# One projection of q instead of two, its features turned by DMA, and kv rows of 66 numbers

## The chip, the cores and the metric

The kernel runs on one core of a Trainium2 chip. The metric is device time in microseconds (us) of one execution; a kernel's time is the median of several executions. A core has five engines that each take their own list of instructions in order: TensorE (PE in the profile; its weight loads are PEld), VectorE (DVE), ScalarE (ACT), GpSimd (POOL) and SyncE (SP). Waits between engines go over semaphores. Transfers are carried by 16 DMA engines; here POOL issues the loads, SP the transposes and the stores.

## The reference

Linear attention with learned features, then a two-layer network with a squared ReLU. Batch 8, 8 heads, 576 positions, head size 64, 128 features; the network is 512 to 2048 to 512 over all 4608 tokens.

```
def phi(x):
    proj = einsum('bhsd,df->bhsf', x, w_phi)
    proj = proj - max(abs(proj), axis=-1, keepdims=True)
    return concatenate([exp(proj), exp(-proj)], axis=-1)
q_p, k_p = phi(q), phi(k)
kv  = einsum('bhsf,bhsd->bhfd', k_p, v)
z   = sum(k_p, axis=2)
num = einsum('bhsf,bhfd->bhsd', q_p, kv)
den = einsum('bhsf,bhf->bhs', q_p, z) + 1e-6
x   = (num / den), heads side by side    # (4608, 512)
out = (max(x @ w_in, 0) ** 2) @ w_out
```

## The kernel before

**Attention, one batch after another.** `attention(b)` handles the 576 positions of a batch as chunks of 128 positions and one of 64, for 8 heads. From batch 2 on, k and q are turned by one DMA transpose each (`transposed`, L326: `kT`, `qT`, 18 blocks of 128x128 each, issued by SP); in batches 0 and 1 TensorE turns them (L316).

For k, a group is projected onto the features (operation Pk, L342, half-height matmuls that run two at a time), DVE takes the largest absolute value (Mk, L397) and ACT makes exp(x) and exp(-x) (Ekp, Ekn, L403, tiles `kp` and `kn`, a ring of `NKP` slots). The maximum goes into `va`, the scaled v, whose rows have room for 66 numbers: 64 of v, the scale that gives the denominator, and one spare. `kv_ops` multiplies `kp` and `kn` with `va` into PSUM (L458, L463), and operation kvc copies the result to `kv_sb`, in rows of 65 numbers (`D1`), 64 of kv and one of z.

For q the projection is made twice. `qmax_ops` projects with the positions on the partitions (Pq, L342), DVE takes the maximum (Mq, L500), and ACT makes exp(-2 max) of it (en). `q_ops` projects once more with the features on the partitions (Fq, L535: two matmuls of 64 rows by 512 columns), and ACT makes exp(x) and exp(-x) from that (L550, tiles `qp` and `qn`). `out_ops` multiplies these with `kv_sb`: eight matmuls with `qp` (NA, L614), the scaling by en on DVE (SA, L626), eight with `qn` on top (NB, L614), a reciprocal (rd, L636), the division (xo, L640), and from batch 1 on a DMA transpose of the result on SP (Xx, L674: `xT`, or `xS` for the chunk of 64), 4 blocks.

**The network.** The 4608 tokens are nine chunks of 512: chunk c is the first 512 positions of batch c, and the ninth is the last 64 positions of all eight batches, collected in `xS`. The first layer is L755 (F1; for chunk 0 the smaller forms f1a, f1b, f1 and f1p at L766, L780 and L794), the ReLU is made by ACT (L732) or DVE (L734), the square by DVE (L741). The second layer is L849 (F2; L813 for the last tile), followed by a copy `ot` on ACT or DVE (L192, L190) and a store on SP (L867, L864).

**The order.** The program makes 1738 operations, each with an engine and planned costs, and then issues them in the order of a list of their numbers, `ORDER`. Each engine's instructions are tied to each other in that order, so the list sets what stands behind what on every engine. `BASES` gives each operation its PSUM bank, `STATES` says for each copy and ReLU whether ACT or DVE makes it, `GATES` makes each load of batch 2 and later on POOL wait for a named operation, and `FILL` puts matmuls on a zero tile (L922, `warm`) ahead of some operations at the start. These tables are the result of an offline search over the planned costs.

Of the kernel before, what the change touches and what calls it, by code (L numbers as in the profile page):

```python
# [107 lines left out]
def kernel(  # L108
# [55 lines left out]
    NKP = 7  # L164
# [4 lines left out]
    kv_sb = ring("kv", 2, [4, 2, 2, D1])  # L169
    NQP = 3  # L170
    NXT = 2
    assert B * S == NCH * TCH and NCH == B + 1 and S == TCH + 64
    qp, qn = ring("qp", NQP, [8 * P]), ring("qn", NQP, [8 * P])
# [4 lines left out]
    mkn = sb("mkn", [36], F32)  # L178
# [120 lines left out]
    kslot, qslot, xslot = [0], [0], [0]  # L299
# [4 lines left out]
    def attention(b):  # L304
# [146 lines left out]
        def kv_ops(pr):  # L451
# [20 lines left out]
            def fn():  # L472
                copy(kv_sb[s2][:, pr].rearrange("f s h c -> f (s h c)"), ps1(g)[:, : 4 * D1])
# [11 lines left out]
        def qmax_ops(c):  # L485
# [17 lines left out]
            add("DVE", dve_cost(2 * n * Fd), fn, r=[pj], w=[("mq", s2, c)], closes=pj, what="Mq")  # L503

# [13 lines left out]
        qfeat = {}  # L518

        def q_ops(c):  # L520
# [21 lines left out]
            for sgn, dst, nm in ((1.0, qp, "qp"), (-1.0, qn, "qn")):  # L542
                def fn(dst=dst, sgn=sgn):
                    i_ = ps2(pf)[:, :, : n * P]
                    if c == 4:
                        o = dst[slot][:, : 8 * 64].rearrange("f (i e x) -> f e i x", e=2, x=P)
                        i_ = i_.rearrange("f e (i x) -> f e i x", x=P)
                    else:
                        o = dst[slot].rearrange("f (e x) -> f e x", e=2)
                    pin(nc.scalar.activation(out=o, in_=i_, func=ACT.Exp, scale=sgn))  # L550
                add("ACT", act_cost(2 * n * P), fn, r=[pf], w=[pf, (nm, slot)],
                    closes=pf if sgn < 0 else None, what="E" + nm)

        def out_halves():
# [4 lines left out]
            for hf in range(2):  # L559
                g = Bank(1, "b0")  # L560
                def heads(sg, g=g, hf=hf):
                    def fn():
                        for u in range(4):
                            h = 4 * hf + u
                            pin(nc.tensor.matmul(
                                out=ps1(g)[:, u * D1 : (u + 1) * D1], lhsT=(qp, qn)[sg][slot][:, h * P : (h + 1) * P],
                                rhs=kv_sb[s2][:, h // 2, sg, h % 2, :], start=(sg == 0 and u == 0),
                                stop=(sg == 1 and u == 3), skip_group_check=True))
                    return fn
# [3 lines left out]
                add("PE", pe_cost(4, 0.0313), heads(0), r=[("qp", slot)] + kvs, w=[g], opens=g, what="NAh")  # L573
# [4 lines left out]
                add("PE", pe_cost(4, 0.0313), heads(1), r=[("qn", slot)] + kvs, w=[g], what="NBh")  # L578
# [21 lines left out]
        def out_ops(c):  # L600
# [4 lines left out]
            slot = qfeat[c]  # L605
# [3 lines left out]
            def heads(sg):  # L609
                def fn():  # L610
                    o = ps2(g)
                    for u in range(8):
# [3 lines left out]
                            lhsT=(qp, qn)[sg][slot][:, u * m : u * m + P],  # L616
                            rhs=kv_sb[s2][:, h // 2, sg, h % 2, :], start=(sg == 0 and u % 4 == 0),
# [3 lines left out]
            add("PE", pe_cost(8, 0.0313), heads(0), r=[("qp", slot)] + kvs, w=[g], opens=g, what="NA")  # L621
# [8 lines left out]
            add("PE", pe_cost(8, 0.0313), heads(1), r=[("qn", slot)] + kvs, w=[g], what="NB")  # L630
# [68 lines left out]
        else:  # L699
# [18 lines left out]
            for c in range(5):  # L718
                qmax_ops(c)
            for c in range(5):  # L720
                q_ops(c)
                out_ops(c)
# [351 lines left out]
```

## Time and profile before

| | |
|---|---|
| median of 3 runs | 353.51 us (353.29 to 354.12) |
| profiled execution, first to last instruction | 351.3 us |
| PE, DVE, ACT busy | 98%, 76%, 67% |
| POOL busy | 27% |
| packets of the loads (queue 0), share of 16 DMA engines | 45.1% |
| packets of SP's transposes and stores (queue 1), the same | 27.2% |
| granted TensorE clock | 1.00 |

The profiled execution is one of its own. The page gives its span, which is 2.2 us under the median of the runs; no other time of it is listed. A busy share is an average over the span. PE's instructions overlap in the pipeline, so what one costs PE is read from the start of one to the start of the next, not from its duration. The rows for SP and for DMA issues show when a transfer was issued and how long it took to land.

### The profile page before, as it was taken

The page shows a single profiled execution, that of the slowest core. Times are in us where ns is not written, and L with a number is a line of the kernel's source. Part 1 is how long each engine was busy: PE and PEld are TensorE (multiplying, and loading weights), DVE is VectorE, ACT ScalarE, POOL GpSimd, SP SyncE. Part 2 cuts the span into 40 slices and gives each one's busy share as a digit, 9 for nine tenths or more (in the row PEclk, how much of TensorE's full clock was granted, in tenths as well). Part 3 has the DMA queues.
Part 4 walks back from the last instruction along what each step waited for, and adds up shares of the span by engine and source line. Part 5 has one row for each costly group of instructions (what it writes and reads, how often), then busy time and mean ns, then how long its engine had stood idle before and what let it go on. Part 6 is the DMA issues. An engine that isn't in the chain of part 4 may idle for free.

```text
span 351.3 us, 8451 instructions
## 1 busy us (share of the span) xinstructions
PE 343.6 (98%) x3402; PEld 193.1 (55%) x3402; DVE 267.2 (76%) x511; ACT 234.9 (67%) x441; POOL 96.2 (27%) x144
## 2 busy tenths in 40 slices
PE   8899999999999999999999999999999999999995
PEld 6789667545655545446555544465555444444443
DVE  5999898999989997898868987998668532645610
ACT  4999998599787885687598857896675612431111
POOL 8827260584509701796013101000000000000000
PEclk9999999999999999999999999999999999999999
DMA  8999999999979999999559774102310113000114
GB/s 104 181 203 197 201 135 129 144 141 179 161 170 155 156 169 193 158 174 134 131 127 106 69 188 80 69 2 61 62 60 10 32 30 124 5 1 29 62 63 116
DMA packets 96117, 39.59 MB, mean 113 GB/s; under 512 B 64592, under 2 KB 91600, under 8 KB 96080
## 3 DMA queue, kind: packets, MB, share of 16 engines
q0 software_dynamic: 45232, 18.36, 45.1%
q1 hardware_dynamic: 50608, 20.55, 27.2%
q8 instruction: 26, 0.43, 0.6%
q10 hardware_dynamic: 240, 0.16, 0.2%
q14 instruction: 11, 0.09, 0.1%
HBM read 36.77 MB, written 9.44 MB: 132 GB/s over the span
## 4 chain that ended last, share of the span: by engine, by line
PE 76%; ACT 12%; DVE 7%; issue 2%; DMA 2%; DVEq 0%; ACTq 0%; POOLq 0%
PE psum L849 31%; PE psum L755 24%; PE psum L614 5%; PE psum L342 4%; PE psum L458 3%; ACT hr L732 2%; PE psum L535 2%; PE psum L794 2%; ACT kp L403 2%; DVE mk L397 2%; DVE h L741 1%; ACT kp L385 1%; DMA xT<-xo 1%; ACT kn L403 1%; ACT kn L385 1%
## 5 line engine op out<-in xcount | busy, mean ns | idle before, releaser
L849 PE MATMUL psum<-wout,h 128*128 128x512 bf16 x560 | 132.6, 379 | 0.1
L755 PE MATMUL psum<-xT,win 128*128 128x512 bf16 x448 | 105.6, 379 | 0.5 <-DVE hr L734 0.2
L732 ACT ACTIVATE hr<-psum 128x512 bf16<-128x512 f32 x101 | 58.3, 596 | 39.0 <-PE psum L755 20.9
L849 PEld LDWEIGHTS <-h 128*128 128x128 bf16 x560 | 51.0, 98 | 55.2 <-issue 0.8
L755 PEld LDWEIGHTS <-win 128*128 128x128 bf16 x512 | 47.2, 98 | 53.5 <-issue 3.4
L741 DVE TENSOR_TENSOR h<-hr 128x512 bf16<-128x512 bf16 x144 | 56.1, 417 | 10.6 <-ACT hr L732 9.6
L734 DVE TENSOR_SCALAR hr<-psum 128x512 bf16<-128x512 f32 x43 | 29.3, 686 | 26.8 <-PE psum L755 26.0
L500 DVE TENSOR_REDUCE mq<-psum 128x8 f32<-128x1024 f32 (+1 forms) x40 | 43.7, 1112 | 6.0 <-PE psum L342 5.7
L550 ACT ACTIVATE qp<-psum 128x1024 bf16<-128x1024 f32 (+1 forms) x40 | 37.5, 939 | 11.5 <-PE psum L535 7.1
L397 DVE TENSOR_REDUCE mk<-psum 128x8 f32<-128x1024 f32 (+1 forms) x35 | 38.6, 1112 | 6.8 <-PE psum L342 6.7
L403 ACT ACTIVATE kp<-psum 128x1024 bf16<-128x1024 f32 (+1 forms) x35 | 32.9, 939 | 15.4 <-DVE mk L397 15.2
L550 ACT ACTIVATE qn<-psum 128x1024 bf16<-128x1024 f32 (+1 forms) x40 | 37.4, 938 | 0.5 <-PE psum L614 0.4
L192 ACT ACTIVATE ot<-psum 128x512 f32<-128x512 f32 x25 | 14.7, 596 | 31.2 <-PE psum L849 29.4
L430 DVE TENSOR_TENSOR va<-xv,va 64x256 bf16<-64x256 bf16 (+2 forms) x66 | 29.8, 474 | 4.8 <-ACT va L416 2.1
L403 ACT ACTIVATE kn<-psum 128x1024 bf16<-128x1024 f32 (+1 forms) x35 | 32.7, 937 | 0.0
L245 POOL DMA_DIRECT2D xv<-in_v_dram x27 | 20.2, 757 | 44.7 <-DVE rden L636 19.1
L626 DVE TENSOR_TENSOR psum<-psum,en 128x520 f32<-128x520 f32 (+1 forms) x39 | 27.2, 699 | 5.3 <-PE psum L614 2.2
L640 DVE TENSOR_TENSOR xo<-psum,rden 128x512 bf16<-128x512 f32 (+1 forms) x39 | 26.7, 687 | 1.0
L245 POOL DMA_DIRECT2D xk<-in_k_dram x28 | 21.2, 768 | 3.6 <-ACT kp L403 2.8
L265 POOL DMA_DIRECT2D xq<-in_q_dram x24 | 17.7, 753 | 9.7 <-ACT qp L550 5.0
L458 PE MATMUL psum<-va,kp 128*128 128x65 bf16 x256 | 19.6, 193 | 0.2
L458 PE MATMUL psum<-va,kn 128*128 128x65 bf16 x256 | 19.6, 193 | 0.0
(82 smaller groups left out, 396.6 us busy)
## 6 DMA issues: line engine op xcount, KB each, us to landing
out_dram<-ot SPq DMA_DIRECT2D x32, 256.0 KB, 2.8
xk<-in_k_dram POOLq DMA_DIRECT2D x26, 128.0 KB, 4.5
xq<-in_q_dram POOLq DMA_DIRECT2D x24, 128.0 KB, 4.8
xv<-in_v_dram POOLq DMA_DIRECT2D x24, 128.0 KB, 4.4
win<-in_moe_w_in_dram POOLq DMA_DIRECT2D x4, 512.0 KB, 12.8
wout<-in_moe_w_out_dram POOLq DMA_DIRECT2D x4, 512.0 KB, 10.8
xq<-in_q_dram POOLq DMA_DIRECT2D x4, 256.0 KB, 6.9
out_dram<-ot SPq DMA_DIRECT2D x6, 128.0 KB, 2.3
```

Of the source, the lines that this page charges most:

```text
L245: pin(nc.gpsimd.dma_start(out=x[:, a * 512 : z * 512].rearrange("p (h x) -> p h x", x=4 * D), in_=src[b][2 * a : 2 * z, 0:512, :].rearrang ...
L397: pin(nc.vector.tensor_reduce(out=mk_view(g), in_=ps2(pj)[:, :, : n * Fd].rearrange("p e (i f) -> p e i f", f=Fd), axis=AX.X, op=ALU.max, ...
L403: pin(nc.scalar.activation(out=dst[slot][:, :, :n, :].rearrange("p e i f -> p e (i f)"), in_=ps2(pj)[:, :, : n * Fd], func=ACT.Exp, scale= ...
L430: pin(nc.vector.tensor_tensor(out=t[:, :, :D].rearrange("p m (x c) -> p m x c", c=2), in0=x.rearrange("p (m x c) -> p m x c", m=n, c=2), i ...
L458: pin(nc.tensor.matmul(out=o[:, sg, hi, :], lhsT=(kp, kn)[sg][kgroup[pr]][:, j % 2, 2 * hi + j // 2, :], rhs=va[s2][sg][:, 8 * pr + 4 * hi ...
L500: pin(nc.vector.tensor_reduce(out=mqb[:, c, :, :n], in_=ps2(pj)[:, :, : n * Fd].rearrange("p e (i f) -> p e i f", f=Fd), axis=AX.X, op=ALU ...
L550: pin(nc.scalar.activation(out=o, in_=i_, func=ACT.Exp, scale=sgn))
L732: pin(nc.scalar.activation(out=hr[sl], in_=ps1(g), func=ACT.Relu))
L734: pin(nc.vector.tensor_scalar(out=hr[sl], in0=ps1(g), scalar1=0.0, scalar2=None, op0=ALU.max))
L741: pin(nc.vector.tensor_tensor(out=dst, in0=i_, in1=i_, op=ALU.mult))
L755: pin(nc.tensor.matmul(out=o, lhsT=win[mc // 4][:, kc, mc % 4 * P : (mc % 4 + 1) * P], rhs=x, start=(kc == 0), stop=(kc == KC - 1)))
L849: pin(nc.tensor.matmul(out=ps1(g), lhsT=h2[c % 2][mc // 4][:, mc % 4, tt * P : (tt + 1) * P], rhs=wout[mc // 4][:, mc % 4, :], start=(mc = ...
```

## The change

From batch 2 on (`TURNED`), q is projected once, with the positions on the partitions. `q_turned` replaces `qmax_ops` and `q_ops` there: the same PSUM result goes to the maximum on DVE and to both exponentials on ACT, which write a tile `qf`, and SP issues a DMA transpose of `qf` into `qpn` (16 blocks of 128x128 for a chunk of 128 positions, 8 for the chunk of 64). `qp` and `qn` become two parts of one tile `qpn`. Batches 0 and 1 keep both projections.

The rows of `kv_sb` get 66 numbers, of which 65 are written and read. `NKP` goes from 7 to 6. The planned cost of one L614 matmul goes from 0.0313 to 0.0297. An unused tile, `mkn`, is dropped.

`ORDER`, `BASES`, `STATES`, `GATES` and `FILL` are new throughout. `FILL` holds 58 fillers where it held 142, and its first 26 stand ahead of another operation (85, a transpose of the last group of k, not 41, the first). POOL's first load is the second half of k of batch 0.

```
-    NKP = 7
+    NKP = 6
...
-    kv_sb = ring("kv", 2, [4, 2, 2, D1])
+    kv_sb = ring("kv", 2, [4, 2, 2, D1 + 1])
...
-    qp, qn = ring("qp", NQP, [8 * P]), ring("qn", NQP, [8 * P])
+    qf, qpn = ring("qf", NQF, [16 * P]), ring("qpn", NQP, [16 * P])     # NQF = 2, NQP = 3
...
-                copy(kv_sb[s2][:, pr].rearrange("f s h c -> f (s h c)"), ps1(g)[:, : 4 * D1])
+                copy(kv_sb[s2][:, pr].rearrange("f s h c -> f (s h) c")[:, :, :D1],
+                     ps1(g)[:, : 4 * D1].rearrange("f (n c) -> f n c", c=D1))
...
+        def q_turned(c):
+            ts = q_ts(c)
+            n = min(len(ts), 4)
+            f, slot = fslot[0] % NQF, qslot[0] % NQP
...
+            pj = project(qTb, "qT", ts, "Pq")
+            def fn():
+                pin(nc.vector.tensor_reduce(
+                    out=mqb[:, c, :, :n], in_=ps2(pj)[:, :, : n * Fd].rearrange("p e (i f) -> p e i f", f=Fd),
+                    axis=AX.X, op=ALU.max, apply_absolute_value=True))
+            add("DVE", dve_cost(2 * n * Fd), fn, r=[pj], w=[pj, ("mq", s2, c)], what="Mq")
+            for sgn, base in ((1.0, 0), (-1.0, 2 * n * P)):
+                def fn(sgn=sgn, base=base):
+                    i_ = ps2(pj)[:, :, : n * Fd]
+                    o = qf[f][:, base : base + 2 * n * P]
...
+                    pin(nc.scalar.activation(out=o, in_=i_, func=ACT.Exp, scale=sgn))
+                add("ACT", act_cost(2 * n * Fd), fn, r=[pj], w=[pj, ("qf", f, sgn)], closes=pj if sgn < 0 else None,
+                    what="Eqp" if sgn > 0 else "Eqn")
+            def fn():
+                pin(nc.sync.dma_start_transpose(out=qpn[slot][:, : 4 * n * P].rearrange("f (t x) -> f t x", x=P),
+                                                in_=qf[f][:, : 4 * n * P]))
+            add("SP", (0.78 + 0.44 * n, 0), fn, r=[("qf", f, 1.0), ("qf", f, -1.0)], w=[("qp", slot), ("qn", slot)],
+                dma=(0.47 * n, HW_IN, "x", "kq"), what="Xf")
+            en_ops(c)
...
-                            lhsT=(qp, qn)[sg][slot][:, u * m : u * m + P],
-                            rhs=kv_sb[s2][:, h // 2, sg, h % 2, :], start=(sg == 0 and u % 4 == 0),
+                            lhsT=qpn[slot][:, sg * half + u * m : sg * half + u * m + P],
+                            rhs=kv_sb[s2][:, h // 2, sg, h % 2, :D1], start=(sg == 0 and u % 4 == 0),
...
-            for c in range(5):
-                qmax_ops(c)
-            for c in range(5):
-                q_ops(c)
-                out_ops(c)
+            if b in TURNED:
+                for c in range(5):
+                    q_turned(c)
+                    out_ops(c)
+            else:
+                for c in range(5):
+                    qmax_ops(c)
+                for c in range(5):
+                    q_ops(c)
+                    out_ops(c)
...
+TURNED = range(2, 8)
```

More of the change, by code (lines that the diff above doesn't have):

```diff
@@ L168 @@
     en = ring("en", 2, [5, 8], F32)
-    kv_sb = ring("kv", 2, [4, 2, 2, D1])
+    kv_sb = ring("kv", 2, [4, 2, 2, D1 + 1])
     NQP = 3
+    NQF = 2
     NXT = 2
     assert B * S == NCH * TCH and NCH == B + 1 and S == TCH + 64
-    qp, qn = ring("qp", NQP, [8 * P]), ring("qn", NQP, [8 * P])
+    qf, qpn = ring("qf", NQF, [16 * P]), ring("qpn", NQP, [16 * P])
     xo = ring("xo", 3, [8 * D])
@@ L177 @@
     xS = sb("xS", [4, KC, P])
-    mkn = sb("mkn", [36], F32)
     hr = ring("hr", 4, [TCH])
@@ L296, in load_wout @@
         add("POOL", (0.72, 0), fn, w=[("wout", i)], dma=(LD["w"], SW_IN, "ld", "first"), what="wout")
-    kslot, qslot, xslot = [0], [0], [0]
+    kslot, qslot, fslot, xslot = [0], [0], [0], [0]
     def t_of(g):
@@ L503, in qmax_ops, with en_ops @@
             add("DVE", dve_cost(2 * n * Fd), fn, r=[pj], w=[("mq", s2, c)], closes=pj, what="Mq")
+            en_ops(c)
+        def en_ops(c):
             if c < 4:
@@ L516, in qmax_ops @@
                     add("ACT", act_cost(4), fn, r=[("mq", s2, 4)], w=[("en", s2, 4, hi)], what="en")
-        qfeat = {}
+        qfeat, qhalf = {}, {}
+        def q_turned(c):
+            ts = q_ts(c)
+            n = min(len(ts), 4)
+            f, slot = fslot[0] % NQF, qslot[0] % NQP
+            fslot[0] += 1
+            qslot[0] += 1
+            qfeat[c], qhalf[c] = slot, 2 * n * P
+            pj = project(qTb, "qT", ts, "Pq")
[8 more added lines that the diff above has]
+                    o = qf[f][:, base : base + 2 * n * P]
+                    if c == 4:
+                        o = o.rearrange("p (i e f) -> p e i f", e=2, f=Fd)
+                        i_ = i_.rearrange("p e (i f) -> p e i f", f=Fd)
+                    else:
+                        o = o.rearrange("p (e x) -> p e x", e=2)
+                    pin(nc.scalar.activation(out=o, in_=i_, func=ACT.Exp, scale=sgn))
[6 more added lines that the diff above has]
+                dma=(0.47 * n, HW_IN, "x", "kq"), what="Xf")
+            en_ops(c)
         def q_ops(c):
@@ L541, in q_ops, with fn @@
             qfeat[c] = slot
-            for sgn, dst, nm in ((1.0, qp, "qp"), (-1.0, qn, "qn")):
-                def fn(dst=dst, sgn=sgn):
+            for sgn, base, nm in ((1.0, 0, "qp"), (-1.0, 8 * P, "qn")):
+                def fn(base=base, sgn=sgn):
                     i_ = ps2(pf)[:, :, : n * P]
                     if c == 4:
-                        o = dst[slot][:, : 8 * 64].rearrange("f (i e x) -> f e i x", e=2, x=P)
+                        o = qpn[slot][:, base : base + 8 * 64].rearrange("f (i e x) -> f e i x", e=2, x=P)
                         i_ = i_.rearrange("f e (i x) -> f e i x", x=P)
                     else:
-                        o = dst[slot].rearrange("f (e x) -> f e x", e=2)
+                        o = qpn[slot][:, base : base + 8 * P].rearrange("f (e x) -> f e x", e=2)
                     pin(nc.scalar.activation(out=o, in_=i_, func=ACT.Exp, scale=sgn))
@@ L565, in fn @@
                             pin(nc.tensor.matmul(
-                                out=ps1(g)[:, u * D1 : (u + 1) * D1], lhsT=(qp, qn)[sg][slot][:, h * P : (h + 1) * P],
-                                rhs=kv_sb[s2][:, h // 2, sg, h % 2, :], start=(sg == 0 and u == 0),
+                                out=ps1(g)[:, u * D1 : (u + 1) * D1], lhsT=qpn[slot][:, sg * 8 * P + h * P : sg * 8 * P + (h + 1) * P],
+                                rhs=kv_sb[s2][:, h // 2, sg, h % 2, :D1], start=(sg == 0 and u == 0),
                                 stop=(sg == 1 and u == 3), skip_group_check=True))
@@ L572, in view @@
                     return ps1(g)[:, : 4 * D1].rearrange("t (h c) -> t h c", h=4)[:, :, :n]
-                add("PE", pe_cost(4, 0.0313), heads(0), r=[("qp", slot)] + kvs, w=[g], opens=g, what="NAh")
+                add("PE", pe_cost(4, 0.0297), heads(0), r=[("qp", slot)] + kvs, w=[g], opens=g, what="NAh")
                 def fn(view=view, hf=hf):
@@ L577, in out_halves @@
                 add("DVE", dve_cost(260), fn, r=[("en", s2, 0, 0)], w=[g], what="SAh")
-                add("PE", pe_cost(4, 0.0313), heads(1), r=[("qn", slot)] + kvs, w=[g], what="NBh")
+                add("PE", pe_cost(4, 0.0297), heads(1), r=[("qn", slot)] + kvs, w=[g], what="NBh")
                 def fn(g=g, hf=hf):
@@ L604, in out_ops @@
             m = 64 if c == 4 else P
-            slot = qfeat[c]
+            slot, half = qfeat[c], qhalf.get(c, 8 * P)
             g = Bank(2, "att")
@@ L620, in out_ops @@
             kvs = [("kv", s2, pr) for pr in sorted({h // 2 for h in head})]
-            add("PE", pe_cost(8, 0.0313), heads(0), r=[("qp", slot)] + kvs, w=[g], opens=g, what="NA")
+            add("PE", pe_cost(8, 0.0297), heads(0), r=[("qp", slot)] + kvs, w=[g], opens=g, what="NA")
             def view(n):
@@ L629, in out_ops @@
             add("DVE", dve_cost(520), fn, r=[("en", s2, c, hi) for hi in range(2 if c == 4 else 1)], w=[g], what="SA")
-            add("PE", pe_cost(8, 0.0313), heads(1), r=[("qn", slot)] + kvs, w=[g], what="NB")
+            add("PE", pe_cost(8, 0.0297), heads(1), r=[("qn", slot)] + kvs, w=[g], what="NB")
             xs = xslot[0] % 3
@@ L717, in attention @@
             kv_ops(3)
-            for c in range(5):
-                qmax_ops(c)
-            for c in range(5):
-                q_ops(c)
-                out_ops(c)
+            if b in TURNED:
+                for c in range(5):
+                    q_turned(c)
+                    out_ops(c)
+            else:
+                for c in range(5):
[3 more added lines that the diff above has]
+                    out_ops(c)
     hslot = [0]
@@ L928 @@
 ORDER = [
[86 rows of a table removed]
[84 rows of a table added]
 ]
 BASES = (
-    '7767715543436622132220767165712404222560646000777103064544450671264242660642446665746753616720006422'
-    '6035462222624260066612617130540005441154060225340064622220424422450561507104611146770464056672022042'
-    '4646026076611077776614577644440604776220206002206404557570466754312356522424247572040002242446247663'
-    '7765645767517617022061671444066420244402207333063071777016326726636542302746113074127362232563074213'
-    '37523'
+    '4547233715671017313424100233242443620720202661650272000142676150354006045660640445514431234333732062'
+    '6546746060000023223732254373253642636003220022660636626275574452255112513141646506744422063604046753'
+    '5134125020754006633435603266604455542425437234542756002002024204064020236322467321743655472423620467'
+    '406052202046645474704177670466344327627237122550443126367420252661033412674'
 )
 STATES = (
-    '0000010111011001001000110000100000000000000000101001011000001010100010000010011101001100100001100000'
-    '1100010010010000100100110001010010001100100000000000010101000000110001000000000100110000000100011001'
-    '0010001010010111011010111100000'
+    '0001000100000001001100011010000000000000010000100011001000001011001000000010000010110001100000100000'
+    '0100101100000000100101000110001010100101000010011100000000000010110000100000010110000111001001110110'
+    '1001110101101001101001101011100'
 )
 GATES = {
[11 rows of a table removed]
[11 rows of a table added]
 }
 FILL = {
-    41: (0, 26), 43: (0, 6), 63: (0, 3), 65: (0, 13), 50: (0, 3), 87: (0, 5), 76: (0, 16), 106: (0, 42), 119: (0,
-    13), 122: (6, 5), 130: (0, 5), 137: (0, 2), 152: (4, 1), 329: (0, 2),
+    85: (0, 26), 87: (0, 4), 43: (5, 4), 65: (7, 7), 116: (5, 6), 137: (4, 6), 139: (0, 5),
 }
+TURNED = range(2, 8)
 STOP = None
```

192 rows, old and new, of tables (GATES, ORDER) are left out of this document.

## The prediction

> **What bounds the kernel now.** I read the page's engine shares first, then the slices, then the groups by shape and the single instructions around the ones that go.
>
> ```profile
> span 351.3 us, 8451 instructions
> PE 343.6 (98%) x3402; PEld 193.1 (55%) x3402; DVE 267.2 (76%) x511; ACT 234.9 (67%) x441; POOL 96.2 (27%) x144
> PE   8899999999999999999999999999999999999995
> DVE  5999898999989997898868987998668532645610
> DMA  8999999999979999999559774102310113000114
> ```
>
> PE is busy from slice 3 to the last, so PE work removed after the start comes off the end, unless a wait replaces it. DVE is close behind it for the first half. DMA is full to about 165 us and nearly idle from 220 us on.
>
> The span leaves 351.3 - 343.6 = 7.7 us without PE, and 142 of its matmuls are fillers. The timeline of PE in the first stretch shows that the start is not PE's:
>
> ```profile
> 0.99 2.95 PE L922 MATMUL psum<-warm 128*128 128x128 bf16 x26 [0.99 <-DVE warm L226]
> 10.32 2.52 PE L922 MATMUL psum<-warm 128*128 128x128 bf16 x42
> ```
>
> From the start times of PE's instructions in the trace, fillers and waits take 16.0 us of the first 30; after that, waits longer than 0.1 us add up to only 2.8 us. The chain of waits in those 30 us is mostly ACT's exponentials (L385: 15.0% and 14.3%). So three pieces make the span: PE's real work (331.5 us by its steps), about 16.0 at the start, and 3.8 after PE's last matmul. They give 351.3; the median of the runs, 353.5, has 2.2 us more around it, which I keep.
>
> **What is removed from PE: the second projection (L535).** Here are single pieces of PE's timeline, start and duration first:
>
> ```profile
> 210.66 0.40 PE L342 MATMUL psum<-wphi,qT 64*128 64x128 bf16 x8
> 210.89 0.38 PE L535 MATMUL psum<-qT,wphi 64*128 64x512 bf16 x2
> 211.11 0.39 PE L342 MATMUL psum<-wphi,qT 64*128 64x128 bf16 x8
> 211.43 2.76 PE L849 MATMUL psum<-wout,h 128*128 128x512 bf16 x12
> ```
>
> The two L535 matmuls of 64 rows run together: from 210.89 to 211.11 they hold PE for 0.22 us (single start times: 0.216), not the 0.38 of one. A pair of 256 columns holds it 0.116. Six batches lose 4 large pairs and 1 small: 24 x 0.216 + 6 x 0.116 = 5.9 us. The last step of a half-height group into full-height matmuls takes 0.309 in place of 0.213, and the full matmul before it 0.312 in place of 0.216: 0.096 at each edge. The old order list has 53 such groups, the new one 57, so 4 x 2 x 0.096 = 0.8 us comes back.
>
> **Rows of 66 numbers.** L614 reads kv rows of 65 bf16, L458 reads va rows that already have 66.
>
> ```profile
> L614 PE MATMUL psum<-kv,qn 128*128 128x65 bf16 x312 | 16.2, 194 | 0.0
> L614 PE MATMUL psum<-kv,qp 128*128 128x65 bf16 x312 | 15.7, 193 | 0.1
> L458 PE MATMUL psum<-va,kn 128*128 128x65 bf16 x256 | 19.6, 193 | 0.0
> ```
>
> The durations are equal, the steps are not: from start to start an L614 matmul takes 29 ns on even heads and 33 to 35 on odd ones, mean 31.1; L458 takes 29 throughout. 640 matmuls (with L565) x (31.1 - 29.1) = 1.3 us. If the pitch is not what makes the odd heads slow, it is 0; I take 1.3, because L458 is the same shape. The copies into kv (ACT 394 ns, DVE 420) write as many numbers as before, so 0.
>
> **What is added: 30 transposes on SP (Xf).** The exponentials and the maximum keep their shapes (1.025 and 1.218 us each) and number, so ACT and DVE pay nothing for the new path. The nearest rows are kT (18 blocks of 128x128) and xT (4 blocks), in the views of these two tiles:
>
> ```profile
> L326 SPq DMA_TRANSPOSE kT<-xk x6: 2679/3198/4240, 59.4 to 202.6; - x6
> DMA to landing us min/median/max: 4.6/5.9/8.3
> ```
>
> ```profile
> L674 SPq DMA_TRANSPOSE xT<-xo x28: 1189/1216/2788, 58.0 to 284.3; - x28
> DMA to landing us min/median/max: 2.3/2.4/5.2
> ```
>
> Between these rows 16 blocks issue in 2.5 us and land after 4.3 / 5.4 / 7.9; each block is 0.16 us more. SP issues 24 x 2.5 + 6 x 1.6 = 70 us more, beside some 100 now (12 at 3.1, 35 at 1.2, 40 stores at 0.5), in a span of 350. It has room, but it is one list: the next kT, qT, xT and output store stand behind each Xf. For the DMA engines, 432 blocks join 342. A block's 128 packets take 18 ns each by the trace, 0.144 us of 16 engines, 62 us in all; if all of queue 1's 27.2% were transposes it would be 0.28 and 121 us. The mean share then rises from 0.73 to between 0.91 and 1.08, where 30 to 170 us ran at 1.17 and 170 to 290 us at 0.37. I take the lower end: the new gates spread the loads into the emptier part.
>
> The Trainium skill speaks against this path: "VectorE: DVE Perf Modes", section "The three transpose paths", gives 1309 ns for a 128x128 block by the DMA crossbar and 390 by TensorE. By it alone the 432 blocks, one after another, would be an estimated 565 us. The kT row disagrees: 18 blocks in 4.6 to 8.3 us is 0.26 to 0.46 each with the fixed part.
>
> What hides Xf: I added up the PE work that the new list has between each turned projection and its first L614. It is 11.8 to 34.7 us. The chain needs 1.2 + 1.0 + 1.0 + 7.9 at the worst, 11.1. So Xf itself costs 0; if that cover were gone, each chunk would wait 4 to 8 us.
>
> What is late next are the others on SP's list. PE work between the issue of kT and the first projection that reads it: 8.4 to 23.9 us in the old list, 5.6 to 7.4 (mean 6.4) in the new. Between a chunk's last xT and its first L755: 6.6 to 8.2 before, 3.1 to 4.3 (mean 3.9) after. In the trace SP issued kT some 1.5 us ahead of its place in the list (mean of six), so these covers are about 7.9 and 5.4, against landings of 5.9 and 2.4 at the median, 8.3 and 5.2 at worst. With a worst landing or two, 0.4 us in all; the bounds are 0 and the slower case below.
>
> **The start.** The new list puts other work ahead of the first L755-like matmul (f1a): adding the rows' durations, ACT has 26.4 us ahead of it where it had 23.8, DVE 27.2 where it had 23.7, PE 9.9 where it had 9.2. At 20 to 30 us of PE work, ACT stands 17.9 us ahead of PE's sum where it was 15.6. ACT's and DVE's rows overlap by about a tenth, so this is 2 us later. Against it stand 84 fewer fillers (58, not 142), 84 x 0.056 = 4.7 us that the new list does not expect to be idle. I take +2.0, with bounds -4.7 and +3.0, since the ACT rows are what the chain goes through there.
>
> **Sum.** 353.5 - 5.9 + 0.8 - 1.3 + 0.4 + 2.0 = 349.5 us. Elsewhere DVE gets 5.0 us more (7 more instructions, six of them the 686 ns relu) and ACT 4.8 less; DVE idles 84 us now, so 0.
>
> **Rivals.** *Front better (0.15).* The fillers tell the truth and the start shortens by up to 4.7 instead of lengthening by 2: 342.8 to 347.5, say 345.
>
> *Slower: SP's queue of transposes (0.23).* For: the chain of waits already has one landing that was late behind two others and a kT.
>
> ```profile
> 66.00 4.41 DMA xT<-xo
> ```
>
> A 16-block Xf ahead in the queue adds 2.6 us to a landing. Then kT lands after 8.5 at the median (0.6 over its cover, six times) and 10.9 at worst (3.0 over); xT after 7.8 at worst (2.4 over, seven chunks). All at the median is 3.6 us, all at worst 35. With one in six at worst, 5.8 + 3.0 = 8.8, the time is 357.9. It decides against the change from 4.4 us of such waits, 0.34 on each of the 13. Against: waits after the start were 2.8 us in all, with twelve such long transposes.
>
> *The pitch does nothing (0.05).* 350.8.
>
> *A cold stretch (0.06).* The first fillers ran at 2.95/26 = 0.113 us each, later ones at 2.52/42 = 0.060, so PE starts at half pace. If the new start, with 84 fewer fillers, leaves a gap that brings this back, the 9 us of real work before the first f1a take up to 9 more; half of it is under ACT's work: 353.5 or so, no change. The granted clock is 1.00 in all windows of this trace, so nothing here shows it. The Trainium skill, "TensorE: Matmul & The Clock Gate", section "Part 1: The HAM clock gate", says that after about 3.4 us of idleness the clock halves; no run here shows that.
>
> *The block price of 1309 ns (0.01).* Over 500 us.
>
> **How the numbers follow.** The forecast holds 0.50, with a range of its own of 347 to 351.5. Faster: 0.50 + 0.15 + 0.05 = 0.70. Same: 0.06. Slower: 0.23 + 0.01 = 0.24. About 0.2% (0.7 us) is what a measurement of this kernel can tell from no change. The range, 344.5 to 357.0, leaves out the far part of the front case and the upper half of the slower one.
>
> **What would show it.** PE's instructions fall by 60 L535 matmuls and 84 fillers; L614 steps of 29 ns on odd heads; the first f1a at 26 to 27 us and not 24.4; about 30 Xf landings of 4.3 to 7.9 us; the waits of PE after 30 us under 4 us. The prediction is wrong if PE's waits on kT or xT pass 4 us, if the slices of PE show a gap after slice 4, or if kT's median landing passes 8 us.

## The result, and the profile after

| | before | after |
|---|---|---|
| median of the runs | 353.74 us (353.29 to 354.12) | 371.95 us (367.88 to 374.06) |
| profiled execution, span | 351.3 us | 369.7 us |
| mean granted clock | 1.00 | 0.972 |

After over before is 1.0459 [1.0415, 1.0503]: 15 to 18 us slower, where 4 us faster were forecast. That ratio leaves out one slow run of after (374.06 us), which the median holds; the medians differ by 18. Further down, differences in us are those of the medians. The runs of after lie up to 6 us apart, so a difference of 1 or 2 us from it shows nothing. The page of after, with the lines that answer to those of before:

```profile
span 369.7 us, 8260 instructions
PE 344.5 (93%) x3258; PEld 192.4 (52%) x3258; DVE 271.4 (73%) x518; ACT 230.5 (62%) x434; POOL 96.2 (26%) x144
PE   6699999979899899998969999899999999999995
DVE  3888998869887599677866998798768853584341
PEclk9859999999999899999998999999999999999999
DMA  9999949999999989999999999999964733100024
q1 hardware_dynamic: 106864, 34.71, 49.5%
q0 software_dynamic: 45232, 18.36, 45.4%
```

PE's row has gaps after slice 4 (the 7, 8, 8, 8, 6 and 8 in the middle), which the row of before hasn't. The DMA row is full for 27 of 40 slices, not 18. The clock row falls below 9 at the start and at two later places. I counted the PE steps of both traces from start to start:

| us of the span | before | after |
|---|---|---|
| real work | 316.2 | 311.1 |
| fillers | 12.1 | 8.4 |
| edges between half- and full-height groups | 9.9 | 11.0 |
| waits and slow steps, 0 to 30 us | 1.7 | 10.8 |
| the same, after 30 us | 6.4 | 22.8 |

So PE does have less to do. Its waits take that and, in these two executions, 18 us more. The view of waits, engines PE and DVE (in all us, times, longest):

```profile
PE psum L797 <- DMA xT<-xo: 5.4, 4, 2.1
PE psum L342 <- DVE xo L677: 3.2, 1, 3.2
PE psum L342 <- DMA kT<-xk: 2.8, 2, 1.4
PE psum L316 <- DVE mk L376: 2.1, 3, 1.2
...
DVE xo L677 <- DMA xT<-xo: 3.5, 1, 3.5
```

After the start nearly all of it is transposes that land late: xT ahead of the first layer (L797, L755 before), kT ahead of the projection (L342). The wait for xo is one of them too: DVE's xo itself waited 3.5 us for an xT. The views of the tiles xT, kT and qpn:

```profile
L326 SPq DMA_TRANSPOSE kT<-xk x6: 2418/2760/5492, 63.4 to 229.3; - x6
DMA to landing us min/median/max: 4.7/5.5/10.3
```

```profile
DMA to landing us min/median/max: 2.4/5.4/8.6
```

```profile
L551 SPq DMA_TRANSPOSE qpn<-qf x30: 1242/2094/5613, 79.1 to 304.3; - x30
DMA to landing us min/median/max: 3.0/4.9/8.0
```

The second view is xT: 5.4 us at the median, where it was 2.4. The new list leaves 5.4 us (by the prediction) to hide it. qpn (Xf) lands after 3.0 to 8.0 and isn't in PE's list of waits: its own cover holds. It is the short covers of others that break.

kT lands no later at the median than in before (5.5 us, where it was 5.9). The two kT that PE waited for were issued late as well: each stands straight behind two Xf and a store in SP's list. The first of them, in the timeline of SP:

```profile
79.13 7.60 SPq L551 DMA_TRANSPOSE qpn<-qf  x2
86.83 0.53 SPq L909 DMA_DIRECT2D out_dram<-ot  x1
87.58 5.49 SPq L326 DMA_TRANSPOSE kT<-xk  x1
```

The rest of the waiting is the clock. PE's timeline at one late xT, and the table by stretch (columns: stretch, length, busy time of PE, PEld, DVE, ACT, POOL, granted clock, DMA share, GB/s):

```profile
117.75 1.03 PE L891 MATMUL psum<-wout,h 128*128 128x512 bf16 x4
119.00 0.59 PE L797 MATMUL psum<-xT,win 128*128 128x512 bf16 x2 [0.22 <-DVE va L430]
121.66 1.01 PE L797 MATMUL psum<-xT,win 128*128 128x512 bf16 x2 [2.07 <-DMA xT<-xo]
```

```profile
10.00:20.00 10.00, 5.98 (x63) 4.67 (x64) 9.17 (x17) 9.47 (x27) 6.43 (x10) 0.78 1.44 186
20.00:30.00 10.00, 9.96 (x129) 8.02 (x127) 6.84 (x15) 7.15 (x15) 5.57 (x8) 0.53 1.41 198
60.00:120.00 60.00, 54.73 (x543) 28.92 (x542) 50.09 (x85) 45.90 (x85) 22.93 (x34) 1.00 1.30 176
120.00:130.00 10.00, 8.25 (x72) 4.11 (x72) 5.86 (x14) 5.62 (x13) 0.70 (x1) 0.83 1.01 179
190.00:200.00 10.00, 6.84 (x45) 3.03 (x44) 3.94 (x5) 6.10 (x11) 2.77 (x5) 0.83 1.54 190
```

At 119 us PE waits 2.07 us for an xT. The clock then halves from 121.5 to 124.9, and two matmuls take 1.01 us where two took 0.59. The other half-speed stretches are 12.3 to 15.7, 19.1 to 29.3 and 193.2 to 196.6 us. In before the records show none up to the end of its work. Both kernels also start at half pace: ahead of the first record of the clock, at 3.9 us in before and 8.9 in after, matmuls of 128 columns step at 107 ns, and at 56 behind it.

### The profile page after: what moved, and what is told of

It reads as the page before. It is cut to its first block, busy times and chain, and to the rows that moved or that the text cites. A ratio compares the mean times of both kernels' runs of the same rounds, so it can differ in the third digit from the quotient of the medians.

```text
span 369.7 us, 8260 instructions
## 1 busy us (share of the span) xinstructions
PE 344.5 (93%) x3258; PEld 192.4 (52%) x3258; DVE 271.4 (73%) x518; ACT 230.5 (62%) x434; POOL 96.2 (26%) x144
## 4 chain that ended last, share of the span: by engine, by line
PE 70%; DMA 14%; DVE 6%; issue 4%; POOL 3%; ACT 1%; SPq 0%; DVEq 0%; POOLq 0%
PE psum L891 24%; PE psum L797 24%; DMA xT<-xo 7%; DMA kT<-xk 5%; PE psum L651 4%; PE psum L458 4%; PE psum L342 4%; PE psum L836 2%; PE psum L316 1%; DMA xS<-xo 1%; DMA xk<-in_k_dram 1%; DVE xo L677 1%; PE psum L808 1%; DVE mq L501 1%; PE psum L855 1%
## 5 line engine op out<-in xcount | busy, mean ns | idle before, releaser
L891 PE MATMUL psum<-wout,h 128*128 128x512 bf16 x560 | 135.4, 382 | 0.0
L797 PE MATMUL psum<-xT,win 128*128 128x512 bf16 x448 | 108.7, 382 | 6.8 <-DMA xT<-xo 5.4
L774 ACT ACTIVATE hr<-psum 128x512 bf16<-128x512 f32 x95 | 54.5, 597 | 56.1 <-PE psum L797 35.1
L797 PEld LDWEIGHTS <-win 128*128 128x128 bf16 x512 | 47.1, 98 | 59.5 <-issue 5.3
L547 ACT ACTIVATE qf<-psum 128x1024 bf16<-128x1024 f32 (+1 forms) x60 | 54.2, 939 | 6.4 <-DVE mq L534 5.3
L776 DVE TENSOR_SCALAR hr<-psum 128x512 bf16<-128x512 f32 x49 | 33.3, 685 | 13.5 <-PE psum L797 12.6
L534 DVE TENSOR_REDUCE mq<-psum 128x8 f32<-128x1024 f32 (+1 forms) x30 | 33.3, 1111 | 6.2 <-PE psum L342 6.0
L192 ACT ACTIVATE ot<-psum 128x512 f32<-128x512 f32 x23 | 13.8, 600 | 38.4 <-PE psum L891 25.9
L651 PEld LDWEIGHTS <-qpn 128*128 128x128 bf16 x624 | 28.4, 98 | 14.4 <-issue 1.7
L651 PE MATMUL psum<-kv,qpn 128*128 128x65 bf16 x624 | 31.6, 194 | 0.1
L265 POOL DMA_DIRECT2D xq<-in_q_dram x24 | 17.4, 724 | 15.7 <-ACT hr L774 5.4
L458 PE MATMUL psum<-va,kp 128*128 128x65 bf16 x256 | 21.2, 199 | 0.0
```

Of the source, the lines that this page charges most:

```text
L458: pin(nc.tensor.matmul(out=o[:, sg, hi, :], lhsT=(kp, kn)[sg][kgroup[pr]][:, j % 2, 2 * hi + j // 2, :], rhs=va[s2][sg][:, 8 * pr + 4 * hi ...
L534: pin(nc.vector.tensor_reduce(out=mqb[:, c, :, :n], in_=ps2(pj)[:, :, : n * Fd].rearrange("p e (i f) -> p e i f", f=Fd), axis=AX.X, op=ALU ...
L651: pin(nc.tensor.matmul(out=o[:, u // 4, u % 4 * D1 : (u % 4 + 1) * D1], lhsT=qpn[slot][:, sg * half + u * m : sg * half + u * m + P], rhs= ...
L774: pin(nc.scalar.activation(out=hr[sl], in_=ps1(g), func=ACT.Relu))
L776: pin(nc.vector.tensor_scalar(out=hr[sl], in0=ps1(g), scalar1=0.0, scalar2=None, op0=ALU.max))
L797: pin(nc.tensor.matmul(out=o, lhsT=win[mc // 4][:, kc, mc % 4 * P : (mc % 4 + 1) * P], rhs=x, start=(kc == 0), stop=(kc == KC - 1)))
```

## The experiments

Three explanations stood against each other: the transposes of the features (Xf) and the loads share the 16 DMA engines, so that all transposes land late; or Xf holds up SP's list by its place in it; or the cold start is the loss. The pitch was tested apart. The expectations give the theories letters of their own, run by run. The runs of before beside these had medians of 353.7 to 354.5 us.

**The pitch alone**, before with rows of 66.

```
-    kv_sb = ring("kv", 2, [4, 2, 2, D1])
+    kv_sb = ring("kv", 2, [4, 2, 2, D1 + 1])
```

> The kernel before with nothing but kv rows of 66 numbers (order and both projections as before). If the odd heads' steps of 33 to 35 ns come from the pitch: all steps of L614 are 29 ns and the time is 352.4 us (1.3 less). If not: 353.7 and the steps stay.

354.44 us, ratio 1.0004 [0.9982, 1.0026]. Odd heads still step at 33 to 35 ns. The pitch is worth nothing.

**The pitch of the product in PSUM**, before with 66 there too.

```
-                            out=o[:, u // 4, u % 4 * D1 : (u % 4 + 1) * D1],
+                            out=o[:, u // 4, u % 4 * (D1 + 1) : u % 4 * (D1 + 1) + D1],
```

> The kernel before with the products of q's features and kv laid in PSUM at a pitch of 66 numbers in place of 65 (kv rows stay at 65). If the odd heads' steps of 33 to 35 ns come from where the product is written: 29 ns throughout and 1.3 us less, 353.1. If not: steps and time as before.

354.13 us, 0.9997 [0.9980, 1.0015], steps unchanged. What slows the odd heads stays open.

**After without the DMAs of Xf.**

```
-                pin(nc.sync.dma_start_transpose(out=qpn[slot][:, : 4 * n * P]...,
-                                                in_=qf[f][:, : 4 * n * P]))
+                pass
```

> The changed kernel without its 30 transposes of q's features; the products with kv read what batches 0 and 1 left in qpn, all else is in place. Theory A (kT, qT and xT come late because Xf stands ahead of them on SP and in the DMA rings): the waits after 30 us fall from 21.5 us to about 6, time 357 us. Theory B (the new order itself is late, loads and DVE): the waits stay, 368 us or more. The start stays cold under both, first f1a at 32 us.

358.22 us, 1.0127 [1.0092, 1.0161]. 13.7 of the 18 us are the Xf DMAs (about 12 of 16 by the ratios), whatever the way. xT still lands after 4.3 us at the median.

**After with Xf cut to one block**: as many issues in the same places of SP's list, 1/16 of the bytes (1/8 for the chunk of 64).

```
-    ...(out=qpn[slot][:, : 4 * n * P]..., in_=qf[f][:, : 4 * n * P]))
+    ...(out=qpn[slot][:, :P]..., in_=qf[f][:, :P]))
```

> The changed kernel with Xf cut to the first of its 16 (or 8) blocks; the rest of qpn keeps what earlier batches left. SP still waits for both exponentials at the same places and PE still waits for Xf. If the volume of Xf (2.5 us of issue and 512 KB each) makes the loss: 358 to 361 us, as without Xf. If SP's standing still at Xf, with kT, xT and stores behind it, makes it: 367 us or more.

362.03 us, 1.0204 [1.0178, 1.0230]. The bytes that are gone are worth 9.9 us, with the shorter issue that comes with them: SP spends 1.15 us on an Xf at the median, where it was 2.1. The 30 short transposes that are left cost 3.8; SP's issues and a fixed part of each transfer are both in that.

**After without the loads of batches 2 to 7**, Xf kept.

```
+                if b >= 2:
+                    return
                 pin(nc.gpsimd.dma_start(
```

> The changed kernel without the loads of k, q and v for batches 2 to 7 (they work on what batches 0 and 1 left); all 30 Xf, kT, qT, xT and stores are in place. Theory E (the 16 DMA engines: transposes are slow while loads run beside them): xT lands after 2.4 to 3 us at the median in place of 5.3, waits of PE over 1 us after 60 us all but vanish, 357 to 360 us. Theory A (SP's own list and ring, whatever else runs): xT stays at 4.5 us or more, 366 us or more.

354.19 us, 0.9980 [0.9958, 1.0002]. With all 30 Xf in SP's list, the tile xT has

```profile
DMA to landing us min/median/max: 2.4/2.5/4.5
```

and 17 of the 28 xT have an Xf in flight beside them: they land after 2.63 us at the median, the other 11 after 2.51. Where an Xf is already in flight when the xT is issued, in 11 cases, it is 2.98 against 2.48. So the place in SP's list is not the cause by itself: an Xf adds 0.1 to 0.5 us, not the 2.6 that the prediction charged.

**After with half the bytes of these loads.**

```
-   ...q[b][2 * y : 2 * y + 2, 0:512, :]...      # two heads a load
+   ...q[b][2 * y : 2 * y + 1, 0:512, :]...      # one; k and v alike
```

> The changed kernel with half of each big load for batches 2 to 7 (one head of two; the other keeps older data). The loads are issued at the same places and kT and qT still wait for them. Theory E (shared DMA engines): the loss falls with the bytes, xT lands after about 3.5 us at the median, 358 to 364 us. Rival (kT and qT are issued late because they wait for loads, and xT behind them; the bytes do not matter): 368 us or more.

357.64 us, 1.0114 [1.0071, 1.0157], xT after 4.0 us at the median. The loss goes with the bytes of the loads as it does with those of Xf, which speaks for the shared engines.

**The start: after with 164 more fillers.**

```
-    85: (0, 26), 87: (0, 4), 43: (5, 4), ...
+    85: (0, 44), 87: (0, 4), 41: (4, 2), 76: (5, 2), 43: (5, 7), 63: (3, 18), ...
```

> The changed kernel with 164 fillers at the start in place of 58, put into the gaps that its trace shows. Theory C (the start is late because PE falls to half clock at 12 and at 19 us): no window of half clock before 30 us, first f1a at 28 to 29 us in place of 32.5, time 368 us. Rival (the start is set by ACT's and DVE's longer lists): first f1a moves by less than 1 us and the time stays at 371 to 372.

370.78 us, 1.0468 [1.0437, 1.0499]. The clock is full from 5 to 155 us and the first f1a comes at 29.2, not 32.5 us, but nothing clear of the noise arrives at the end: 1.2 us by the medians, none by the ratios. There are half-speed stretches at 155 and 193 us behind late transfers instead.

**The same fillers where less is late**: without Xf,

> The changed kernel without Xf and with the 164 fillers at the start. Alone, the fillers took 3.3 us off the first f1a and only about 1 off the time. If the rest was given back to transfers that are late with Xf, it now stays: 354.5 to 356 us against 358.2 without Xf alone. If the start is worth nothing anyway: 358.

and without the loads.

> The changed kernel without the loads of k, q and v for batches 2 to 7 and with 164 fillers at the start. Without those loads it took 354.2 us with its cold start. If the start is a second cause that stands by itself, the 3 us that the fillers save now reach the end: 351 us, 3 under the kernel before. If it is given back: 354.

356.10 us (1.0042 [1.0023, 1.0060]), 2.1 less than without these fillers; and 351.58 us (0.9931 [0.9915, 0.9948]), 2.6 less (3.0 and 1.7 by the ratios). The cold start is a second cause of some 2 to 3 us. With Xf and all loads in place it is given back to later waits. As the main cause it falls. The kernel without loads leaves out work, so its time is only a bound.

**Thirty idle transposes in before**, of Xf's sizes, from `wout` to one scratch tile.

```
+            pin(nc.sync.dma_start_transpose(out=scr[:, : n * P]..., in_=wout[u % 4]...))
+        add("SP", (0, 0), fn, what="idle")
```

> The kernel before, with 30 idle transposes of the size of Xf on SP (from wout into a scratch tile that nothing reads), each released where the second exponential of a q chunk ends, at least 4.8 us of PE work apart. Both projections stay. Theory A in the form that the short covers of the new order are needed for the loss: the old covers of 8 to 24 us for kT and 7 us for xT hold, time 354 to 358 us. Rival (the DMA engines are full, so that 432 more blocks cost the same in any order): 364 us or more.

398.69 us, 1.1272 [1.1236, 1.1308]. The rival's 364 or more came, but by a flaw of the edit. The view of waits, engine SP:

```profile
SPq L915 <- DMA scr<-wout: 36.7, 13, 8.4
```

With one scratch tile each idle transpose waits on SP for the one before it, and stores and xT stand behind that. It shows how dear a waiting SP is, and doesn't separate the engines from the list.

**Xf only where few loads are left**: before's order with eight late chunks turned (of batches 5 to 7), first with the maximum behind the exponentials,

```
+TURNED = [(5, 0), (5, 2), (5, 4), (6, 1), (6, 2), (7, 0), (7, 1), (7, 4)]
```

> The kernel before in its own order (kv rows of 65, seven kp slots), with eight of the 40 chunks turned by DMA: those of batches 5 to 7 that the old order gives at least 5 us of other work between their exponentials and their first product, late enough that few loads are left. The maximum comes after the exponentials, and one qf tile serves all. If the loss needs loads beside the transposes: 8 x 0.2 us saved on PE, 352.5 to 353.5 us. If Xf delays kT and xT even so: 356 us or more.

then with it ahead of them.

> This is the kernel of the run with eight late chunks (old order; chunks 0, 2 and 4 of batch 5, 1 and 2 of batch 6, 0, 1 and 4 of batch 7 projected once and their features turned by DMA), with the maximum and en at once after the projection, ahead of the exponentials, as the change has it, and not behind them. Theory A, that the transposes of the features do harm only where they share the DMA engines with loads: these eight lie where few or no loads run, so the loss of that run was its own wait of DVE for the exponentials; the time falls to 352.5 to 353.5, up to 8 x 0.2 = 1.6 us under before, if DVE doesn't now wait for the projection instead. Theory B, that a single 16-block transpose in the old order does harm by its own latency or by its place in SP's list: 356 or more again, with PE waiting on qpn, xT or kT. Should the time stay high with DVE waiting for the projection, the place of the maximum in a list that was planned without it is the cause, and the run says nothing of the two.

363.74 us (1.0273 [1.0256, 1.0291]) and 363.85 us (1.0275 [1.0258, 1.0293]). xT lands after 2.5 us at the median in both, and PE waits for no transpose after the start. It waits for ACT, and ACT for the maximum, which stands elsewhere in DVE's list than the old order had it. The view of waits of the second:

```profile
ACT en L510 <- DVE mq L532: 9.3, 6, 3.4
...
ACT qf L545 <- DMA qpn<-qf: 3.2, 2, 2.7
...
PE psum L793 <- ACT ot L192: 2.8, 2, 2.2
PE psum L793 <- ACT hr L770: 2.3, 5, 0.9
PE psum L342 <- ACT qf L545: 1.8, 3, 0.9
```

ACT also waits for an Xf itself, 3.2 us in two waits, because one qf tile serves all eight. So these two don't tell what Xf costs beside few loads; they show that this order, searched for other operations, doesn't bear the new ones.

**Are the new gates to blame?** I counted, from issues and landings, how many loads are in flight over the first 2.4 us of each xT. In before 0.5 on average, and 2 of the 28 have 2.5 or more; in after 3.8, and 16 have. These 16 land after about 7 us (6 issued with no Xf in flight 6.9, 10 with one 7.1), the 8 with no load after 2.7. Without Xf the gates of after still put 14 xT beside 2.5 loads or more, and these land after 5.5. So I gave the loads other places and gates: none from 3.8 us before to 2.3 us after an xT, 1.1 us apart, everything else as in after.

```
 GATES = {
-    ..., 574: 222, 575: 206, 576: 272, ...
+    ..., 574: 264, 575: 208, 576: 260, ...       # all from about 46 us on, ORDER to match
```

> The changed kernel with all of its transposes of the features; only the places and gates of the loads from about 46 us on are other ones: each is released by a PE operation such that it isn't issued from 3.8 us before to 2.3 us after an xT transpose, 1.1 us apart. Theory G, that the loss after the start is that loads are in flight beside the xT transposes, because the new gates release them there: xT lands after 2.5 to 3.5 us at the median, PE's waits on xT and the falls of the clock behind them go, and the time is 355 to 360 (354.2 is the kernel without these loads). Theory V, that the volume of the transposes of the features and of the loads is too much for the DMA engines wherever the loads stand: 365 or more, with waits on kT, qT, qpn or xv in place of those on xT.

> The kernel with the loads kept away from the xT transposes, and the 164 fillers at the start besides. Theory G: 2 to 3 us less than without these fillers, 352.5 to 358, as in the two runs in which no transfer was late (2.1 and 2.6 us). Theory V: no more than 1.2 us less, as in the run with late transfers.

> As the kernel with loads kept away from xT and with the fillers, but the loads stand 0.9 us apart, and none is issued within 2 us of the issue of kT either. Theory G, if kT is what is late next: 1 to 3 us under the kernel with the fillers and without this, with kT's worst landing under 8 us. If kT isn't late there, no difference or a little slower, since the loads then stand closer together.

388.25 us (1.0978 [1.0924, 1.1033]); with the fillers 386.60 (1.0928 [1.0880, 1.0976]); with the fillers and loads off kT too, 0.9 us apart, 387.58 (1.0912 [1.0860, 1.0964]). Of the first, the waits of PE, and the landings of xT, kT and qpn in this order:

```profile
PE psum L342 <- DMA kT<-xk: 16.0, 4, 7.0
PE psum L651 <- DMA qpn<-qf: 5.4, 3, 3.5
```

```profile
DMA to landing us min/median/max: 2.4/2.6/4.6
```

```profile
DMA to landing us min/median/max: 4.7/8.9/13.7
```

```profile
DMA to landing us min/median/max: 3.1/6.4/10.4
```

xT is as early as in before, as the theory of the gates (G) has it, and the kernel is 16 us slower still. The loads that no longer meet xT now meet Xf and kT. Is that the crowding, or bad places? The same places without Xf:

> The kernel with the loads kept away from the xT transposes, without the DMA of the 30 transposes of the features (the multiplications read what stands in that tile, so the output is not that of the reference). Theory V, that loads and these transposes together are too much wherever they stand: without them the places do no harm, kT lands under 8 us, and the time is 353 to 359 (358.2 is the changed kernel without these transposes, with its own gates). Theory P, that the places themselves are bad, since the loads stand closer together beside kT: 365 or more, with PE still waiting for kT by more than 6 us.

357.21 us, 1.0084 [1.0055, 1.0114], no wait for kT over 0.5 us. The places do no harm by themselves; Xf costs 31 us in them, and 13.7 in those of the new list. That speaks for the volume (V): in the two placements that were run, the loads, Xf and kT don't fit together, and the gates choose only which of them is late.

SP's list has a part in it that V leaves out. The landings of kT without Xf:

```profile
DMA to landing us min/median/max: 4.7/7.7/9.9
```

With Xf the median is only 1.2 us more, 8.9. But PE reaches for a kT 11.0 us after its issue without Xf, on the mean of the six, and 6.9 us after it with Xf, because then Xf stand ahead of kT in SP's list. Each of them takes SP 3.0 us to issue at the median, where it took 1.9 in the kernel without loads. So crowding makes landings later and issues longer, and both reach kT. How the loss divides between the engines and the list was not separated. A list that spreads both better was not searched for, and no version that does the whole work was faster than before.

## Why the prediction was wrong

- **PE's saving: right.** Real work fell by 5.1 us and edges rose by 1.1; forecast were 5.9 and 0.8. Without the loads of batches 2 to 7 and with the fillers at the start the kernel takes 351.58 us. Against 349.5 that is 1.3 for the pitch, and 0.8 besides, which the first f1a at 29.0 and not 26 to 27 us can account for.
- **The pitch: wrong, 0 for 1.3.** The rival that held this (350.8) was right on that point. L458 has the same shape and rows of 66, but that row alone didn't make the pitch the cause.
- **The start: wrong in size.** The first f1a came 8.1 us later (24.44 to 32.51), against +2.0. The cold-stretch rival, given 0.06, took place: recorded half clock for 13.6 of the first 30 us, and half pace for 5 us longer at the start. The argument that the granted clock is 1.00 in before's trace fails, because before has 84 fillers more. Even with 164 fillers and full clock the first f1a comes at 29.0 to 29.4 us, some 4.7 later than in before, so the new order's own part was over the +2.0 too. The fillers are worth 2 to 3 us at the end, and only where less is late further on.
- **Late transfers, the step that failed: 0.4 us.** PE's waits and slow steps after 30 us rose by 16.4 us. Three steps led there. The landings of a quiet queue (xT 2.4) were set against the new covers, with a worst case or two. The mean DMA share was put at its lower end, 0.91 to 1.08: it came to 0.95 (0.495 + 0.454), and Xf to 79.6 us of the 16 engines (0.495 x 369.7 less 28.8% of 359.2 without Xf), inside the bounds of 62 and 121. So the volume was sized rightly; but "I take the lower end" then charged nothing for it, as if engines that are full on average gave every transfer its quiet time. And "the new gates spread the loads into the emptier part" was half right: the share went from 0.26 to 0.98 between 200 and 290 us, but between 60 and 200 it rose as well, from 1.03 to 1.26.
- **The slower rival (0.23, 357.9)** named the right waits, kT and xT, and the right turning point: 16.4 us is well over its 4.4. Its price came from the wrong cause, a landing made 2.6 us later by the Xf ahead of it, which is 0.1 to 0.5 us without loads; it left the loads out. Xf ahead in SP's list does harm by making kT's issue later, which it didn't price. The 16.4 us lie between its 8.8 and its bound of 35.
- **What would show it**: the removed PE instructions came as said, and Xf's landings (3.0 to 8.0 us, forecast 4.3 to 7.9) nearly so; the steps of 29 ns on odd heads and the first f1a at 26 to 27 us did not. Two of the three signs against it came: waits on transposes of over 4 us, and gaps in PE's row after slice 4. kT's median landing, 5.5 us, stayed under 8.

The Trainium skill, "DMA: Bandwidth & Descriptors", section "Rules for kernel authors", says that DMAs from different issuing engines all run on the same 16 DMA engines and interleave. The runs agree: SP's xT lands after 2.5 us without POOL's loads and after 5.4 with them. Its clock rule, in "TensorE: Matmul & The Clock Gate", "Part 1: The HAM clock gate", gives half clock after a window of some 3.4 us of idleness. The runs agree on the length (the stretches are 3.4 and 10.2 us), but not on the idleness, as the last section shows.

## What to carry to other kernels

Before moving work from an engine to DMA, add up by stretch what the DMA engines then carry, beside what is already there, and expect waits wherever the sum rises in a stretch that was already full. Here transfers got late there, and those with the shortest cover paid first, not the added ones. Ask also what stands behind the added transfers in their issuer's list. A landing time read from a quiet queue is a lower bound; look in the trace at how many loads were in flight beside it. Filling a gap at the start gave little here while a later transfer ended last, and moving the loads away from one victim made another.

## What the runs showed of the hardware that was not expected

- An xT transpose of 4 blocks lands after 2.3 to 2.7 us at the median with no load in flight (before, after, and after without Xf or without loads). With 2.5 loads or more in flight, mostly of 128 KB, it lands after 5.5 us without Xf in the kernel and after 7.1 with it. An Xf in flight beside it adds 0.1 to 0.5 us where there are no loads.
- Issuing slows as well: kT's issue on SP took up to 5.5 us in after (4.2 before), Xf's 1.2 to 5.6 (1.2 to 3.5 without the loads).
- The clock halves without an idle window. In the 3.4 us ahead of the four half-speed stretches of after, PE was busy for 1.69, 1.52, 1.28 and 0.70 us by the trace; one wait of 2.07 us among short work was enough. Each 3.4 us at half speed then costs up to 1.7 us on top of the wait.
- Matmuls of 65 columns with kv step at 29 ns on even heads and 33 to 35 on odd ones with rows of 65 or 66 numbers in SBUF, and with 66 in PSUM.
